# Moving the old-state products behind a unit's first scores, with new figures in the planner

## The chip, the cores and the metric

The kernel runs on one core of a Trainium2 chip. The metric is the device time in microseconds (us), median of the runs. TensorE is called PE, VectorE DVE, ScalarE ACT, GpSimd POOL; SP is the engine that issues most loads.

## The reference

A linear attention with a decaying state (4 batches, 8 heads, 768 steps, head size 48), then a gated projection with a convolution of five taps. Cut to what is computed:

```python
for t in range(S):
    cur = einsum('bhd,bhe->bhde', u[None] * kt, vt)
    y[:, :, t] = einsum('bhd,bhde->bhe', rt, state + cur)
    state = wt[:, :, :, None] * state + einsum('bhd,bhe->bhde', kt, vt)
# x = y with the heads side by side: (4, 768, 384)
for k in range(5):
    gate_pre += conv_w[k] * xp[:, k:k + S, :]
gate = 1 / (1 + exp(-gate_pre))
out = (gate * (x @ w_val)) @ w_out
```

## The kernel before

**Units.** Two heads form a pair, 16 pairs in all. A pair's 768 steps are cut into six chunks of 128 steps, each of two halves of 64. A unit is a pair, or part of one: 21 units, of which the first pair has two (two and four chunks), the pairs 1 to 11 one of six chunks each (units 2 to 12), and the last four pairs two each (four and two chunks).

**What a unit does.** `unit_front`: SP loads w, k and r (`rkw`); DVE scans the decays (`g` at L410, `f` at L437), and POOL (DVE in the first units) makes scaled keys `kh` and queries `q`; ACT makes `ru`, r times the bonus. `unit_state`: PE transposes the keys (L469), ACT copies them out (`kt`, L473), PE makes the state updates `pu` (L485) and those of the half chunks (L499), DVE chains them into states `st` (L524), PE adds the middle ones (L533), and ACT copies both into `z` (L546). `unit_scores`: PE multiplies the old states with the queries, `earlier` (L559), into the output bank `py`, and makes the scores in the bank `pp` (L580); DVE copies the wanted triangle and diagonal into `am` with two masked copies (L592). `unit_back`: PE adds `am` times v to `py`, `outputs` (L601), and ACT evacuates `py` into `xt` or, for every fourth pair, `ys` (L618). There is one bank pair for `pp` and one for `py`, so scores of one part wait for the masks of the part before, and `earlier` waits for the evacuation of the unit before.

**Parts.** A unit of six chunks makes scores and outputs in two parts of three chunks (`parts`); the smaller units have one part.

**The gate stage.** Whenever four pairs of a batch are done, two chunks of 384 steps of the gate stage are put in: taps on ACT and DVE (L695, L697), the two projections on PE (L636).

**The order.** All of this is written down as operations with an engine, a cost in ns and keys read and written (`r`, `w`). `Schedule.times` simulates the engines: at each step the engine that can start first takes, of its ready operations, the one with the longest rest of work behind it. `emit` then issues all of them by simulated start. So costs and keys decide only the order in which each engine gets its instructions; the waits between engines follow from the tiles. The key `py` in the scores' `r` is such an ordering: scores don't touch that bank. SP's operations are chained in the written order. `TensorClock` models PE's clock in the plan: double cost while it reckons PE as not warm, by the share of a model window in which PE was busy.

Of the kernel before, what the change touches and what calls it, by code (L numbers as in the profile page):

```python
# [19 lines left out]
B, H, S, D = 4, 8, 768, 48  # L20
# [34 lines left out]
def dve(n):  # L55
    return 75 + 1.042 * n


def scan(n):
    return 75 + 2.084 * n  # L60


def act(n, psum=False):
    return (60 if psum else 100) + 0.833 * n
# [10 lines left out]
class TensorClock:  # L75
# [6 lines left out]
        self.k, self.busy, self.warm = 0, 0.0, False  # L82

    def turn(self):
        self.warm = self.busy > (0.42 if self.warm else 0.9) * self.W
        self.k, self.busy = self.k + 1, 0.0

    def run(self, t, cost):
# [123 lines left out]
def rwkv_moe(ctx, tc, rkw, pad_d, vn_d, wv_d, wo_d, cw_d, small_d, out):  # L212
# [634 lines left out]
    op = ops.op  # L847
    units = [Unit(u) for u in range(NU)]

    def load(k, cost, fn, *args, w):  # L850
        op("SP", 470 * k, fn, *args, w=w)
        op("DMA", cost, None, w=w + ["loads"])

    def unit_v(u):
        load(1, 273 * units[u].n, load_v, u, w=[("vn", u % 4)])

    def unit_front(u, what="work"):
        a = units[u]
        n, i2, i3, rkk = a.n, u % 2, u % 3, ("rk", u % 4)
        rk_pad = [rkk, ("pad", u % 4)]  # L860
        N = n * L
        if what == "load":
            return load(2, 414 * n, load_rkw, u, w=[rkk])
        op("DVE", scan(N), a.scan_g, r=rk_pad + ["e1"] + ["e1b"] * (u > 0), w=["g"], port=True)
        op("DVE", 130, a.inverse, r=["g"], w=[("d1", i2)])
        op("Act", 110, a.totals, r=["g"], w=[("tot", u)])
        e, c = ("DVE", dve(N)) if u in DVE_KEYS else ("Pool", pool(N))
        op(e, c, a.keys, r=["g"] + rk_pad, w=[("kh", i3)], port=True)
        op("DVE", scan(N), a.scan_f, r=rk_pad + [("d1", i2)], w=[("f", i2)], port=True)
        e, c = ("DVE", dve(N)) if u in DVE_QUERIES else ("Pool", pool(N))  # L870
        op(e, c, a.queries, r=rk_pad + [("f", i2)], w=[("q", i3)], port=True)
        op("Act", act(N) + 188, a.guard, r=rk_pad + ["wmin"], w=[("ru", i3), ("low", u)])
        op("Act", act(N) + 93, a.bonus, r=rk_pad + ["masks"], w=[("ru", i3)])

    def unit_state(u):
        a = units[u]
        n, i2, i3 = a.n, u % 2, u % 3
        for j0 in range(0, n, 3):
            k = min(3, n - j0)
            pt = ("pm", ops.turn("pm", 2))  # L880
            op("PE", 104 * k, a.transpose, j0, r=[("kh", i3), "masks"], w=[pt])
            op("Act", act(112 * k, True), a.transposed, j0, r=[pt], w=[("kt", i2, j0)])
        kts = [("kt", i2, j0) for j0 in range(0, n, 3)]
        pu = ("pm", ops.turn("pm", 2))
        op("PE", 60 + 118 * a.slots, a.updates, r=kts + [("vn", u % 4)], w=[pu])
        ibk = ("ib", ib_key(u))
        op("Act", act(D * (n - 1)), a.decay, r=[("tot", u), "ibs"], w=[ibk])
        if a.late:
            op("Act", 150, a.carried, r=[("carry", a.p), pu], w=[pu])
        pu0 = ("pm", ops.turn("pm", 2))  # L890
        op("PE", 60 + 118 * n, a.halves, r=kts + [("vn", u % 4)], w=[pu0])
        op("DVE", scan(D * a.slots) + 60, a.chain, r=[pu, ibk], w=[("st", u % 4)] + [("carry", a.p)] * a.more)
        op("Act", act(D * n), a.state, 0, r=[("st", u % 4)], w=[("z", i2, 0)])
        op("PE", 60 + 40 * n, a.middle, r=[("st", u % 4), "masks"], w=[pu0])
        op("Act", act(D * n, True), a.state, 1, r=[pu0], w=[("z", i2, 1)])

    def unit_scores(u):
        a = units[u]
        n, i2, i3 = a.n, u % 2, u % 3
        op("PE", 60 + 232 * n, a.earlier, r=[("z", i2, 0), ("z", i2, 1), ("q", i3)], w=["py"])  # L900
        for i, j0 in enumerate(a.parts):
            op("PE", 60 + 240 * a.step, a.scores, i, w=["pp"],
               r=[("kh", i3), ("q", i3), ("ru", i3), ("rk", u % 4), "py"])
            N = 2 * a.step * 64
            for what in range(2):
                op("DVE", dve(N) + 60, a.mask, i, what, r=["pp", "masks"], w=[("a", i2, i)])

    def unit_back(u):
        a = units[u]
        i2, b, hp, n = u % 2, a.p // 4, a.hp, a.n  # L910
        for i, j0 in enumerate(a.parts):
            op("PE", 60 + 120 * a.step, a.outputs, i, r=[("vn", u % 4), ("a", i2, i)], w=["py"])
        own = [("x", b % 2, hp, c) for c in range(a.c0, a.c0 + n)]
        spare = [("xs", b % 2, c) for c in range(a.c0, a.c0 + n)]
# [88 lines left out]
    for u in range(NU):  # L1003
        a = units[u]
# [15 lines left out]
    op("Act", 2200, first_sigmoid, r=["warm"], boost=1e6)  # L1020
    for i in range(WARM):
        op("PE", 213, warm_up, 1, r=["warm"], w=[("pf", 0)], boost=-1e6)
    for i in range(4):
        op("Act", 600, load_pad, i, w=[("pad", i)])
        op("DMA", 240, None, w=[("pad", i)])
    unit_front(0, "load")
    load(1, 530, load_small, w=["masks"])
    unit_front(1, "load")
    unit_v(0)
    unit_front(2, "load")  # L1030
    unit_v(1)
    load(1, 50, load_taps, w=["cwr"])
    unit_front(3, "load")
    unit_v(2)
    unit_v(3)
# [24 lines left out]
    for u in range(NU):  # L1060
# [20 lines left out]
        p, c0, n = UNITS[u]  # L1081
# [79 lines left out]
```

## Time and profile before

| | us |
|---|---|
| median of 3 runs | 300.29 (298.99 to 301.29) |
| profiled execution | 301.02 |
| its span, first to last instruction | 299.2 |
| PE busy | 250.8 (84%) |
| DVE busy | 201.2 (67%) |
| ACT busy | 152.6 (51%) |
| POOL busy | 118.9 (40%) |

The profile is of one execution. Busy time is the time in which an engine had an instruction in hand; the ends of matmuls are modelled, so a busy PE is not PE at its peak. Two rows of PE matmuls can overlap. The granted clock is the share of full speed (2.4 GHz) that PE was given in a stretch. An idle time is put down to what ended it.

### The profile page before, as it was taken

How to read it: one execution, taken by the hardware profiler on the slowest of the kernel's cores; microseconds unless marked ns; L12 is line 12 of the kernel's file. 1: busy time of each engine (PE TensorE's matmuls, PEld its weight loads, DVE VectorE, ACT ScalarE, POOL GpSimd, SP SyncE). 2: the span in 40 equal slices, each digit the busy share in tenths (PEclk: the TensorE clock that was granted, in tenths of full speed). 3: DMA queues.
4: the chain of work that ended last, by engine and by line, in shares of the span. 5: the costliest groups of instructions: out<-in, count | busy, mean ns of one | idle time of the engine just before them, and what ended most of it. 6: DMA issues, size and time to landing. Idle time of an engine off the chain costs nothing. (4 is left out here: it accounts for less than half of the span.)

```text
span 299.2 us, 10120 instructions
## 1 busy us (share of the span) xinstructions
PE 250.8 (84%) x4411; PEld 213.2 (71%) x4411; DVE 201.2 (67%) x325; ACT 152.6 (51%) x347; POOL 118.9 (40%) x114
## 2 busy tenths in 40 slices
PE   7559988988689995899999899899689967966873
PEld 2448777767577874788788798699578956845762
DVE  2746867759985598788298797548597854577300
ACT  1645535353436484464485955634585743664211
POOL 8035226236327338705263771515263223061210
PEclk9655575555555899599999999979997995897798
DMA  7999976244542671552861533273222100100011
GB/s 146 174 182 301 261 160 121 45 82 83 110 92 53 110 129 36 104 137 59 149 151 37 110 76 113 61 149 92 65 57 79 56 15 3 61 22 26 26 53 64
DMA packets 13381, 28.81 MB, mean 96 GB/s; under 512 B 2192, under 2 KB 8208, under 8 KB 12208
## 3 DMA queue, kind: packets, MB, share of 16 engines
q1 hardware_dynamic: 8784, 21.58, 34.9%
q10 hardware_dynamic: 4544, 6.50, 7.7%
q8 instruction: 36, 0.59, 0.9%
q14 instruction: 17, 0.14, 0.2%
HBM read 22.17 MB, written 4.72 MB: 90 GB/s over the span
## 5 line engine op out<-in xcount | busy, mean ns | idle before, releaser
L697 DVE SCALAR_TENSOR_TENSOR acc<-xt,cw,acc 128x384 f32<-128x384 f32 (+1 forms) x108 | 61.4, 569 | 16.1 <-ACT acc L695 14.5
L410 DVE TENSOR_TENSOR_SCAN g<-rkw,e 112x774 f32<-112x774 f32 (+2 forms) x21 | 34.5, 1643 | 25.8 <-DMA rkw<-rkw 25.5
L592 DVE COPY_PREDICATED am<-small,pp 128x384 f32<-128x384 int32 (+2 forms) x64 | 37.4, 584 | 21.5 <-PE pp L580 21.4
L717 POOL TENSOR_TENSOR gl<-gt,gh 128x384 fp32r<-128x384 f32 (+1 forms) x27 | 27.1, 1002 | 61.8 <-ACT gh L713 61.8
L432 POOL TENSOR_TENSOR kh<-rkw,g 112x768 f32<-112x768 f32 (+2 forms) x19 | 28.1, 1477 | 40.3 <-PE pp L580 20.7
L446 POOL TENSOR_TENSOR q<-rkw,f 112x768 f32<-112x768 f32 (+2 forms) x20 | 28.3, 1413 | 31.4 <-DVE f L437 31.4
L559 PE MATMUL py<-q,z 48*48 48x64 f32 (+1 forms) x704 | 31.7, 253 | 8.7 <-ACT xt L618 5.7
L559 PEld LDWEIGHTS py<-q,z 48*48 48x48 f32 (+1 forms) x704 | 28.2, 156 | 13.1 <-ACT xt L618 6.3
L437 DVE TENSOR_TENSOR_SCAN f<-rkw,d 112x774 f32<-112x774 f32 (+2 forms) x21 | 32.5, 1548 | 0.2
L458 ACT ACTIVATE ru<-rkw,wmin 112x768 f32<-112x768 f32 (+2 forms) x21 | 16.4, 783 | 26.5 <-PE pp L580 15.7
L683 POOL TENSOR_TENSOR xl<-xt,xh 128x1152 fp32r<-128x1152 f32 (+2 forms) x11 | 21.6, 1968 | 18.7 <-ACT xh L679 17.3
L485 PE MATMUL pu<-vn,kt 128*64 128x48 f32 (+1 forms) x404 | 20.2, 253 | 10.0 <-DMA vn<-vn 5.2
L485 PEld LDWEIGHTS pu<-vn,kt 128*64 128x64 f32 (+1 forms) x404 | 17.4, 161 | 14.6 <-issue 7.1
L580 PE MATMUL pp<-q,kh 48*64 48x64 f32 x768 | 24.5, 258 | 3.1 <-issue 1.8
L710 DVE TENSOR_TENSOR gt<-gt,pv 128x384 f32<-128x384 f32 (+1 forms) x27 | 13.6, 502 | 19.5 <-PE pv L636 14.1
L636 PE MATMUL pv<-xh,wv_hi 128*128 128x384 f32 (+1 forms) x81 | 20.9, 369 | 6.0 <-DVE gt L710 4.7
L636 PE MATMUL po<-wo_hi,gh 128*128 128x384 f32 x72 | 22.1, 418 | 4.5 <-ACT ob L728 2.7
L601 PE MATMUL py<-am,vn 64*64 64x64 f32 (+1 forms) x768 | 22.4, 256 | 2.5 <-DVE am L592 2.5
L601 PEld LDWEIGHTS py<-am,vn 64*64 64x64 f32 (+1 forms) x768 | 18.0, 155 | 9.0 <-DVE am L592 5.1
L728 ACT COPY ob<-po 128x384 f32<-128x384 f32 x24 | 11.5, 479 | 24.8 <-PE po L636 19.2
L580 PEld LDWEIGHTS pp<-q,kh 48*64 48x64 f32 x768 | 19.5, 161 | 6.2 <-issue 3.6
L580 PE MATMUL pp<-ru,rkw 48*64 48x64 f32 x768 | 23.2, 252 | 0.0
(83 smaller groups left out, 477.1 us busy)
## 6 DMA issues: line engine op xcount, KB each, us to landing
rkw<-rkw SPq DMA_DIRECT2D x22, 435.9 KB, 7.2
out<-ob ACTq DMA_DIRECT2D x24, 192.0 KB, 2.0
vn<-vn SPq DMA_DIRECT2D x11, 288.0 KB, 6.2
rkw<-rkw SPq DMA_DIRECT2D x10, 290.8 KB, 5.1
rkw<-rkw SPq DMA_DIRECT2D x10, 145.7 KB, 2.9
xt<-wv SPq DMA_DIRECT2D x3, 384.0 KB, 10.3
raw_o<-wo SPq DMA_DIRECT2D x3, 384.0 KB, 13.3
vn<-vn SPq DMA_DIRECT2D x5, 192.0 KB, 2.9
```

The lines of the kernel that those rows point to most:

```text
L410: nc.vector.tensor_tensor_scan(self.g[:, 0:m][:, ::-1], w[:, 1 : m + 1][:, ::-1], e1[:, 0:m][:, ::-1], 0.0, op0=ALU.mult, op1=ALU.add,)
L432: eng.tensor_tensor(self.kh[:, 0:n, :], k, slots(self.g, n)[:, :, 1:WS], op=ALU.mult)
L437: nc.vector.tensor_tensor_scan(self.f[:, 0:m], rk(u)[:, 0, 0:m], d1[u % 2][:, 0:m], 0.0, op0=ALU.mult, op1=ALU.add)
L446: eng.tensor_tensor(self.q[:, 0:n, :], r, slots(self.f, n)[:, :, 0:L], op=ALU.mult)
L485: nc.tensor.matmul(self.pu[64 * h : 64 * h + rows, :, k], self.kt[:, c, 64 * h : 64 * h + rows], vn_t[u][:, c, 48 * h : 48 * h + 48], star ...
L559: nc.tensor.matmul(self.py[64 * h : 64 * h + m, j, 64 * c : 64 * c + 64], z_t[u % 2][ps, (2 * c + j) * D : (2 * c + j) * D + m], self.q[ps ...
L580: nc.tensor.matmul(pp[t, h, 128 * c + b : 128 * c + b + 64], lh[ps, j0 + c, t], rh[ps, j0 + c, t], start=True, stop=True,)
L592: nc.vector.copy_predicated(am, bm(mdia if what else mstr, step), p5[:, :, :, what, :])
L601: nc.tensor.matmul(self.py[64 * h : 64 * h + m, j, 64 * c : 64 * c + 64], vn_t[u][t, c, 48 * h : 48 * h + m], am[t, h, c, :], start=False, ...
L636: nc.tensor.matmul(ps, lh(a, cc), rh(bb, cc), start=(m == 0), stop=(m == 8))
L697: nc.vector.scalar_tensor_tensor(self.acc[j], x, w, self.acc[j], op0=ALU.mult, op1=ALU.add)
L717: nc.gpsimd.tensor_tensor(self.gl[:, j, 0:n], self.gt[:, j, 0:n], self.gh[:, j, 0:n].bitcast(F32), op=ALU.subtract)
```

## The change

In units of two parts the old-state products are written between the first and the last scores instead of ahead of both, and only the last scores carry the ordering key `py`. The outputs are written with the last part first. Six figures of the planner change: the busy share from which it reckons PE as warm (0.9 to 0.97), the time of a v load (273 to 230 ns a chunk), of an rkw load (414 to 727 ns a chunk), of a pad load (240 to 700 ns, now in one chain with the other loads), and of the copy of the states into z (340 to 705 ns for six chunks). The pad loads are written between the first units' loads instead of all ahead of them.

```diff
     def turn(self):
-        self.warm = self.busy > (0.42 if self.warm else 0.9) * self.W
+        self.warm = self.busy > (0.42 if self.warm else 0.97) * self.W
...
     def unit_v(u):
-        load(1, 273 * units[u].n, load_v, u, w=[("vn", u % 4)])
+        load(1, 230 * units[u].n, load_v, u, w=[("vn", u % 4)])
...
         if what == "load":
-            return load(2, 414 * n, load_rkw, u, w=[rkk])
+            return load(2, 727 * n, load_rkw, u, w=[rkk])
...
-        op("Act", act(D * n), a.state, 0, r=[("st", u % 4)], w=[("z", i2, 0)])
+        op("Act", 100 + 2.1 * D * n, a.state, 0, r=[("st", u % 4)], w=[("z", i2, 0)])
...
     def unit_scores(u):
         a = units[u]
         n, i2, i3 = a.n, u % 2, u % 3
-        op("PE", 60 + 232 * n, a.earlier, r=[("z", i2, 0), ("z", i2, 1), ("q", i3)], w=["py"])
         for i, j0 in enumerate(a.parts):
+            if i == len(a.parts) - 1:
+                op("PE", 60 + 232 * n, a.earlier, r=[("z", i2, 0), ("z", i2, 1), ("q", i3)], w=["py"])
             op("PE", 60 + 240 * a.step, a.scores, i, w=["pp"],
-               r=[("kh", i3), ("q", i3), ("ru", i3), ("rk", u % 4), "py"])
+               r=[("kh", i3), ("q", i3), ("ru", i3), ("rk", u % 4)] + ["py"] * (i == len(a.parts) - 1))
...
-        for i, j0 in enumerate(a.parts):
+        for i in reversed(range(len(a.parts))):
             op("PE", 60 + 120 * a.step, a.outputs, i, r=[("vn", u % 4), ("a", i2, i)], w=["py"])
...
-    for i in range(4):
+    def pad(i):
         op("Act", 600, load_pad, i, w=[("pad", i)])
-        op("DMA", 240, None, w=[("pad", i)])
+        op("DMA", 700, None, w=[("pad", i), "loads"])
+
+    pad(0)
     unit_front(0, "load")
     load(1, 530, load_small, w=["masks"])
+    pad(1)
     unit_front(1, "load")
     unit_v(0)
+    pad(2)
     unit_front(2, "load")
     unit_v(1)
     load(1, 50, load_taps, w=["cwr"])
+    pad(3)
     unit_front(3, "load")
```

## Rows read from the trace of the kernel before

**Rows 1.** The page, part 2: granted clock in 40 slices of 7.5 us, tenths.

```profile
PEclk9655575555555899599999999979997995897798
```

**Rows 2.** Stretches: us, each engine's busy us (instructions), granted clock, DMA share, GB/s.

```profile
0.00:20.00 20.00, 12.35 (x101) 6.82 (x103) 8.60 (x17) 6.97 (x19) 7.26 (x31) 0.76 0.97 167
...
40.00:42.00 2.00, 2.00 (x51) 1.88 (x48) 1.04 (x2) 0.00 (x0) 0.00 (x0) 0.73 1.01 196
...
46.00:99.00 53.00, 45.47 (x873) 39.17 (x866) 41.65 (x54) 25.49 (x52) 23.77 (x17) 0.50 0.47 88
64.00:84.00 20.00, 14.35 (x289) 12.36 (x290) 20.00 (x25) 10.36 (x22) 9.96 (x6) 0.50 0.61 113
...
126.00:192.00 66.00, 63.18 (x1347) 55.50 (x1346) 50.65 (x81) 40.01 (x85) 28.41 (x21) 1.00 0.43 98
240.00:299.00 59.00, 41.70 (x387) 35.61 (x383) 25.01 (x58) 22.66 (x56) 14.30 (x16) 0.84 0.10 34
```

**Rows 3.** PE's waits, 20 to 100 us: us in total, times, longest.

```profile
PE py L601 <- DVE am L592: 1.9, 1, 1.9
...
PE py L559 <- ACT xt L618: 1.0, 1, 1.0
PE py L559 <- ACT ys L618: 0.9, 1, 0.9
...
PE pp L580 <- DVE am L592: 0.5, 1, 0.5
```

**Rows 4.** PE's waits, 100 to 195 us.

```profile
PE py L559 <- ACT ys L618: 1.4, 2, 1.0
PE py L559 <- ACT xt L618: 0.9, 1, 0.9
...
PE pp L580 <- DVE am L592: 0.8, 2, 0.6
```

**Rows 5.** Timeline, 82 to 100 us: start, us, instruction, count, idle before.

```profile
82.91 2.50 PE L559 MATMUL py<-q,z 48*64 48x64 f32 x42 [0.93 <-ACT ys L618]
...
85.80 1.74 DVE L410 TENSOR_TENSOR_SCAN g<-rkw,e 112x774 f32<-112x774 f32 x1
85.90 0.89 PE L580 MATMUL pp<-ru,rkw 48*64 48x64 f32 x22
...
87.46 0.57 DVE L592 COPY_PREDICATED am<-small,pp 128x384 f32<-128x384 int32 x1
...
90.23 1.52 PE L485 MATMUL pu<-vn,kt 128*64 128x48 f32 x24 [0.53 <-ACT kt L473]
...
94.61 0.60 DVE L592 COPY_PREDICATED am<-small,pp 128x384 f32<-128x384 int32 x1 [2.05 <-PE pp L580]
...
95.62 0.58 DVE L592 COPY_PREDICATED am<-small,pp 128x384 f32<-128x384 int32 x1
...
96.30 0.91 PE L601 MATMUL py<-am,vn 64*64 64x64 f32 x24
...
99.81 1.43 PE L559 MATMUL py<-q,z 48*64 48x64 f32 x43
```

**Rows 6.** The page's DMA issues (KB each, us to landing), and one ACT copy.

```profile
rkw<-rkw SPq DMA_DIRECT2D x22, 435.9 KB, 7.2
...
rkw<-pad ACTq DMA_DIRECT2D x4, 145.3 KB, 7.8
...
87.82 0.71 ACT L546 COPY z<-st 112x288 f32<-112x288 f32 x1
```

**Rows 7.** Timeline of DVE around 20 us.

```profile
19.07 1.77 DVE L410 TENSOR_TENSOR_SCAN g<-rkw,e 112x774 f32<-112x774 f32 x1 [4.33 <-DMA rkw<-rkw]
20.76 0.42 DVE L592 COPY_PREDICATED am<-small,pp 128x256 f32<-128x256 int32 x1
```

**Rows 8.** Timeline of PE, two instructions behind a gap.

```profile
45.34 0.81 PE L580 MATMUL pp<-q,kh 48*64 48x64 f32 x20 [1.77 <-issue]
...
194.29 1.44 PE L559 MATMUL py<-q,z 48*64 48x64 f32 x28 [1.02 <-ACT ys L618]
```

## The prediction

> **What bounds the kernel now.** I read the page first. Its row of the granted TensorE clock stands at 5 to 7 tenths from the second slice to the thirteenth (to about 97 us), nearly always at the lower of the two levels, 1.2 GHz, and mostly at 9 behind it [rows 1]. So I cut the span into stretches. From 46 to 99 us PE is busy 45.47 of 53 us, all of it at 0.50; from 126 to 192 us it is busy 63.18 of 66 us at 1.00 [rows 2]. PE is the fullest engine in both, but they differ in what is left: 7.5 us of idle time in the first, 2.8 in the second. Inside the first lies 64 to 84 us, where VectorE has no idle time at all while PE has 5.65 us of it: there masks come late because DVE is full. After 240 us PE is busy 41.70 of 59 us; that is mostly the last batch's gate and projection, which the new order does not touch.
>
> Then I asked what PE waited for. From 20 to 100 us the idle time is split over many small waits: the products with the old states (L559) wait 1.0 + 0.9 us for an evacuation of the unit before, the scores 0.5 us for a mask, the outputs 1.9 us for a mask [rows 3]. From 100 to 195 us L559 waits 1.4 + 0.9 us and the scores 0.8 us [rows 4].
>
> Last, one round of the loop from unit to unit, at the low clock [rows 5]. L559 of one unit starts at 82.91, after 0.93 us of waiting for ACT's evacuation. The first scores follow and end at 86.79. Their first mask starts on DVE only at 87.46, because a scan g of 1.74 us stands before it. The next unit's updates fill PE at 90.23. The masks of the second scores start at 94.61 and 95.62, the outputs at 96.30, and the next L559 at 99.81. The round takes 16.9 us, and two pairs of masks and one evacuation stand in it one behind the other.
>
> **The change part by part.**
>
> *L559 moves behind the first scores.* In a unit of six chunks it is 44 matmuls, which pass 24 + 24 matmuls of scores on PE; no DMA goes with them, and on the other queues nothing is passed. Units of two or four chunks have one part, so their order stays. Two waits should go. L559 no longer meets an unfinished evacuation, since the first scores, which don't write py, run in that time: about 1.3 us of them (85.4 to 86.79) against waits of about 1 us [rows 5]. And the second scores no longer meet unfinished masks, since L559 now runs in that time: 2.50 us at the low clock, 1.43 us at the high one, against a pair of masks of 2 x 0.58 us. The terms: from 20 to 100 us 1.0 + 0.9 + 0.5 = 2.4 us [rows 3]; from 100 to 195 us 1.4 + 0.9 + 0.8 = 3.1 us [rows 4], less the 1.0 at 194.29, whose 28 matmuls show a unit of four chunks [rows 8]: 2.1 us. Together 4.5 us. The lower bound is 0 (the same idle time comes back at the next wait); the upper is all of PE's idle time in the two stretches, 7.5 + 2.8 = 10.3 us. I take 4.5, the waits that the new order names, because PE is the fullest engine around them.
>
> *Both parts' outputs now come after the last scores, the second part first.* Before, the first part's outputs (0.9 us at the low clock) could run while the second masks were made. Now all 48 matmuls wait for the last mask, which ends at 96.20, 1.6 us after the masks could begin; with the way back to PE that is some 1.7 us per unit [rows 5], and the evacuation and the next L559 are queued behind. The work that hides it is the next unit's transposes, updates, halves and middle products; the updates alone are 1.52 us at the low clock [rows 5], and the four together over 3. I take 0. If that cover stood somewhere else, it would be 11 units x 1.7 = 19 us, the other bound.
>
> *Loads reckoned dearer, v cheaper, one copy dearer.* The planner's rkw load goes to 727 ns a chunk, 4.36 us for a unit of six whose two transfers of 435.9 KB landed in 7.2 us each; z from st goes to 100 + 2.1 x 288 = 705 ns, which the trace has at 0.71 [rows 6]. No work comes with this, only another order. SP keeps the written order of its loads, since the planner chains them, so no load passes another. What it can do is seen at the start: DVE waited 4.33 us for unit 2's load with unit 0's masks queued behind that scan [rows 7]. A plan that knows the load to be late puts the masks first, which takes one mask, 0.42 us, out of the way of unit 1's states, and unit 0's outputs as well. Between 0 and 1.1 us; I take 0.5.
>
> *Pads.* The four pad transfers of 145.3 KB are issued from ACT [rows 6]. Their issues wait for nothing in either plan, so I cost the new place at 0. If two of them really went behind the first unit's loads, these would land earlier by 2 x 145.3 KB at the 167 GB/s of that stretch [rows 2], 1.7 us: the upper bound.
>
> *A stricter clock in the planner* only makes it reckon with slow matmuls for longer, and that reorders every engine, in the tail too. No row prices it. The nearest are PE's single waits that an order can make or remove, the longest of them 1.9 us outside the start [rows 3]; so 1.9 us either way, and I take 0.
>
> Sum: 4.5 + 0.5 = 5.0 us off the profiled execution's 301.02 (a span of 299.2 and 1.8 around it), 296.0. That execution stood 0.73 us above the median of the runs, 300.29, so the forecast is 300.29 - 5.0 = **295.3 us**.
>
> **The rivals.**
>
> *The clock rises early.* PE was granted 0.73 in 40 to 42 us [rows 2], behind a stretch of scores and updates, and lost it in a gap that ended at 45.34 [rows 8]. Scores, L559 and scores in one piece make a longer dense stretch in every unit. At the high level L559 would fall from 2.50 to 1.43 us [rows 5], PE would bound 46 to 99 us no longer, and DVE, with 41.65 us of work there [rows 2], would: some 45 us in place of 53, a gain of 8 where the first case has 2.4. That gives 300.29 - 8 - 2.1 - 0.5 = 289.7, about 290. Against it: 45.47 busy us out of 53 did not raise the clock, and DVE's full stretch will go on making gaps. The Trainium skill (TensorE: Matmul & The Clock Gate, "What's actually happening") has the throttled state as the default, which activity releases. By that rule denser work would bring this case; the trace agrees at 40 us and speaks against counting on it by the 53 us at 0.50.
>
> *Nothing net.* The waits of L559 and the scores go, and the same idle time stands at the outputs or, from 64 to 84 us, behind DVE. Or the planner finds the first scores ready no sooner than the old products, and the change hardly does what it says. Either way about 299.5.
>
> *Slower: the outputs lose their cover.* If the plan puts the next unit's state work ahead of the second scores, little stands between these and the outputs, and evacuation, L559 and everything after slide. For it speak the 1.9 us that the outputs wait already [rows 3], and the 1.74 us scan that DVE ran before a mask [rows 5]. From 5.0 / 11 = 0.45 us uncovered per unit on, the gain is gone. With the 1.7 us uncovered in half of the 11 units it is 9.4 - 5.0 = 4.4 us slower than before, about 305. Against it: both waits of that kind in the two stretches add up to little over 2 us, since something nearly always stood between.
>
> **How the numbers follow.** Waits removed, clock as before (292 to 298): 0.42. Clock early (284 to 292): 0.20. Nothing net (298 to 302): 0.18. Slower (302.5 to 310): 0.20. The time is that of the first, 295.3. A range of 285 to 304 leaves out the lowest end of the clock case (0.03) and the upper part of the slow one (0.13), and takes in the bounds of the small terms. About 1%, 3 us, can be told from no change. Faster than 297.3 are 0.8 of the first case and the whole clock case: 0.54. Slower than 303.3 is nearly all of the last: 0.20. Within it: 0.26.
>
> **What would show it.** Right: from 20 to 195 us L559 waits for an evacuation only in units of four chunks or fewer, the scores' waits for masks vanish, and the outputs' waits for masks stay under 3 us. The clock case: a granted clock above 0.6 over much of 46 to 99 us. Slower: outputs waiting over 8 us for masks. I am wrong in the place, whatever the total, if the difference arises after 240 us, where I put none, or before 20 us beyond half a microsecond.

## The result and the profile after

The changed kernel takes 289.65 us (median of 4 runs, 286.49 to 293.44) beside 300.79 us of the kernel before (4 runs, 298.99 to 305.29): a ratio of 0.958 [0.946, 0.969]. (A ratio compares undisturbed runs alone, so it need not be the quotient of the two medians.) A second measurement of the same file gave 287.38 us and 0.964 [0.953, 0.975]. The forecast was 295.3 us; the time lies inside its range, and the gain is about twice the one forecast.

The profiled execution took 288.46 us, its span 286.7 us. The page's first two parts, of the changed kernel:

```profile
PE 237.6 (83%) x4411; PEld 204.3 (71%) x4411; DVE 201.5 (70%) x325; ACT 152.6 (53%) x347; POOL 121.9 (43%) x114
...
PEclk9855555596557999999699999999986999978998
```

No engine has less to do: DVE is busy 201.5 us (201.2 before) and ACT 152.6 us, as before. PE is busy 237.6 us in place of 250.8, with the same matmuls, because more of them ran at the high clock. The row of the granted clock reaches its run of 9s one slice earlier than in [rows 1].

To see where the time went, both spans are cut where the same work begins: at the old-state products (L559) of unit 5 and of unit 13. The views of stretches, first of the kernel before, then of the changed one (columns as in [rows 2]: us, then busy us and instructions of PE, weight load, DVE, ACT and POOL, granted clock, DMA share, GB/s):

```profile
0.00:82.90 82.90, 65.50 (x1108) 52.44 (x1108) 57.19 (x81) 37.49 (x84) 32.86 (x47) 0.58 0.74 151
82.90:194.30 111.40, 101.90 (x2121) 88.14 (x2121) 84.42 (x128) 65.10 (x135) 54.86 (x35) 0.90 0.44 94
194.30:299.20 104.90, 83.44 (x1184) 72.59 (x1184) 59.58 (x117) 50.00 (x129) 31.21 (x32) 0.88 0.19 55
82.90:299.20 216.30, 185.34 (x3303) 160.73 (x3303) 144.00 (x245) 115.10 (x263) 86.07 (x67) 0.89 0.32 75
```

```profile
0.00:82.90 82.90, 58.60 (x1107) 46.84 (x1107) 55.08 (x81) 37.02 (x83) 32.15 (x47) 0.63 0.80 158
82.90:187.70 104.80, 97.19 (x2079) 85.73 (x2079) 88.83 (x127) 63.71 (x131) 58.30 (x36) 0.93 0.45 97
187.70:286.70 99.00, 81.82 (x1227) 71.70 (x1227) 57.55 (x118) 51.87 (x134) 31.45 (x33) 0.92 0.18 56
82.90:286.70 203.80, 179.01 (x3306) 157.43 (x3306) 146.38 (x244) 115.57 (x265) 89.75 (x68) 0.93 0.32 77
```

Three things are to be seen. Unit 5 begins at 82.9 us in both, with 1107 and 1108 matmuls done: the first third gained nothing. The whole 12.5 us lie behind it: 6.6 us up to unit 13, 5.9 us after it. (At unit 13 the changed kernel has some 40 matmuls of the next unit's state work still ahead of it, 2079 against 2121; that is over 1 us which the middle owes the tail, so the split between the two is rough, while the sum is not: 3303 and 3306 matmuls.) And of these 12.5 us half is idle time, half is busy time: PE sat idle 216.30 - 185.34 = 31.0 us before and 203.80 - 179.01 = 24.8 us after, 6.2 us less; it was busy 6.3 us less, at a granted clock of 0.93 in place of 0.89.

**What became of the waits.** PE's waits between unit 5 and unit 13 of the kernel before, then of the changed one (us in total, times, longest; L559's for xt and the scores' for masks are as in [rows 4]):

```profile
PE pu L533 <- DVE st L524: 2.7, 1, 2.7
PE py L559 <- ACT ys L618: 2.3, 3, 1.0
PE py L601 <- DVE am L592: 0.6, 1, 0.6
```

```profile
PE pp L580 <- DVE am L592: 4.5, 2, 2.7
PE py L559 <- ACT z L546: 2.8, 2, 2.6
PE pu L485 <- ACT kt L473: 1.6, 3, 0.5
PE py L601 <- DVE am L592: 0.5, 1, 0.5
```

No old-state product waits for an evacuation there any more, and the outputs wait as little as before. But the scores' wait for masks did not vanish: it is 4.5 us in two pieces. (The view counts a wait with the instruction that it delays. Of the waits for ys and for z, 0.93 and 2.56 us stand right before unit 5's own old-state products, at 82.91 and 82.88 us, and so ahead of the cut; the middle itself has 0.2 us for z.) All of PE's idle time in this stretch fell only from 9.5 us (111.40 - 101.90) to 7.6 us (104.80 - 97.19). One unit of the changed kernel on PE shows the new order and one of the two pieces:

```profile
105.19 0.56 PE L580 MATMUL pp<-q,kh 48*64 48x64 f32 x24
...
106.46 1.49 PE L559 MATMUL py<-q,z 48*64 48x64 f32 x44
107.95 0.90 PE L485 MATMUL pu<-vn,kt 128*64 128x48 f32 x24
108.78 0.90 PE L499 MATMUL pu<-vn,kt 64*64 64x48 f32 x24
111.46 0.58 PE L580 MATMUL pp<-q,kh 48*64 48x64 f32 x24 [1.79 <-DVE am L592]
```

First scores, old-state products, next unit's updates and halves, second scores (and, at 114.63 us, both parts' outputs in one row of 48): the move is done as the diff says. Even with 1.49 + 0.90 + 0.90 us of work between the two scores, PE waited 1.79 us for the masks. DVE's timeline shows what stood before them, here and at the longer piece, 2.72 us at 137.37 us; two rows of POOL stand ahead of it:

```profile
105.09 3.22 POOL L683 TENSOR_TENSOR xl<-xt,xh 128x1152 fp32r<-128x1152 f32 x1 [2.98 <-ACT xh L679]
108.26 3.02 POOL L446 TENSOR_TENSOR q<-rkw,f 112x768 f32<-112x768 f32 x1
...
106.30 0.59 DVE L592 COPY_PREDICATED am<-small,pp 128x384 f32<-128x384 int32 x1
106.78 3.16 DVE L410 TENSOR_TENSOR_SCAN g<-rkw,e 112x774 f32<-112x774 f32 x1
...
110.83 0.57 DVE L592 COPY_PREDICATED am<-small,pp 128x384 f32<-128x384 int32 x1
...
136.17 0.55 DVE L710 TENSOR_TENSOR gt<-gt,pv 128x384 f32<-128x384 f32 x1 [2.85 <-ACT gt L700]
136.65 0.58 DVE L592 COPY_PREDICATED am<-small,pp 128x384 f32<-128x384 int32 x1
```

The two masked copies of one part are 4.5 us apart, with a scan of 3.16 us and steps of the gate stage between; and at 136 us the second copy is queued behind a gate step that itself waits 2.85 us for ACT. The same scan took 1.74 us in [rows 5], with nothing on POOL beside it; here xl and q run on POOL all through it.

**What a wait costs.** The granted clock shows where the other half came from. The stretches around two of the changed kernel's longest waits behind 100 us, and the timeline's rows of these waits:

```profile
131.00:138.00 7.00, 4.28 (x140) 3.79 (x142) 3.54 (x7) 2.17 (x6) 3.46 (x3) 0.99 0.31 78
138.00:145.00 7.00, 7.00 (x105) 6.26 (x102) 5.29 (x7) 4.49 (x7) 5.92 (x3) 0.52 0.38 89
206.00:213.00 7.00, 4.61 (x83) 3.82 (x82) 6.67 (x13) 5.82 (x13) 4.94 (x5) 1.00 0.22 59
213.00:220.00 7.00, 6.70 (x102) 6.07 (x102) 3.69 (x6) 2.61 (x7) 1.20 (x2) 0.51 0.06 20
```

```profile
137.37 0.58 PE L580 MATMUL pp<-q,kh 48*64 48x64 f32 x24 [2.72 <-DVE am L592]
...
213.30 1.75 PE L559 MATMUL py<-q,z 48*64 48x64 f32 x28 [2.02 <-ACT z L546]
```

Ahead of 138 us PE had the high level, 2.4 GHz (0.99), and sat idle 2.72 us of 7; in the 7 us behind, it was busy without a break at 0.52, nearly all at the low level of 1.2 GHz. The same stands around 213 us (1.00, a wait of 2.02 us, then 0.51). The kernel before has it too, with another wait: at 119.17 us the middle products wait 2.66 us for states, and 119.5 to 126.5 us runs at 0.51. A single long wait thus stands ahead of a slow stretch, and where the one brings the other, it costs its own length and half of that stretch's busy time, here, by an estimate, (1 - 0.52) x 7.00 = 3.4 us. The Trainium skill (TensorE: Matmul & The Clock Gate, "HAM oscillation — how this bites in real kernels") tells of a kernel whose every wait for data is followed by matmuls at the low clock; both traces agree at these places. But it does not come behind every wait here: in the kernel before one of 2.63 us, at 212.99 us, has 213 to 220 us behind it at 1.00, though PE was busy only 4.37 of the 7 us ahead. And in a second execution of the changed kernel (below) the wait for masks near 137 us, 2.13 us there, has 7 us behind it at 1.00. So which waits bring a slow stretch differs between executions of one program.

**The tail.** The last outputs (L601) of the kernel before start at 260.15 us, with 324 of the gate stage's 459 projection matmuls (L636) done, and 38.6 us are left behind their end. Those of the changed kernel start at 267.23 us, with 387 done, and 19.0 us are left. So the changed plan runs 63 more of them ahead of the last outputs. That stretch has units of one part only, in which the move changes nothing by itself; the planner, which plans all of the program anew, placed them so.

### The profile page after: what moved, and what is told of

It reads as the page before. It is cut to its first block, busy times and chain, and to the rows that moved or that the text cites. A ratio compares the mean times of both kernels' runs of the same rounds, so it can differ in the third digit from the quotient of the medians.

```text
span 286.7 us, 10120 instructions
## 1 busy us (share of the span) xinstructions
PE 237.6 (83%) x4411; PEld 204.3 (71%) x4411; DVE 201.5 (70%) x325; ACT 152.6 (53%) x347; POOL 121.9 (43%) x114
## 4 chain that ended last, share of the span: by engine, by line
PE 58%; ACT 12%; DVE 10%; DMA 10%; issue 4%; ACTq 3%; SPq 1%; POOL 1%; DVEq 0%; POOLq 0%
PE po L636 14%; PE pv L636 11%; PE pp L580 8%; PE py L559 8%; DMA rkw<-rkw 5%; PE pu L485 5%; PE pu L499 4%; PE py L601 4%; DVE acc L697 3%; DMA vn<-vn 3%; PE pt L469 3%; ACTq L627 3%; PE pu L533 2%; DMA xt<-ys 2%; DVE am L592 2%
## 5 line engine op out<-in xcount | busy, mean ns | idle before, releaser
L717 POOL TENSOR_TENSOR gl<-gt,gh 128x384 fp32r<-128x384 f32 (+1 forms) x27 | 29.0, 1076 | 49.8 <-ACT gh L713 49.8
L410 DVE TENSOR_TENSOR_SCAN g<-rkw,e 112x774 f32<-112x774 f32 (+2 forms) x21 | 38.4, 1831 | 11.6 <-DMA rkw<-rkw 11.5
L559 PE MATMUL py<-q,z 48*48 48x64 f32 (+1 forms) x704 | 29.9, 245 | 11.9 <-ACT z L546 6.3
L432 POOL TENSOR_TENSOR kh<-rkw,g 112x768 f32<-112x768 f32 (+2 forms) x19 | 26.8, 1410 | 30.1 <-PE pp L580 15.5
L559 PEld LDWEIGHTS py<-q,z 48*48 48x48 f32 (+1 forms) x704 | 26.7, 149 | 16.6 <-ACT z L546 7.9
L683 POOL TENSOR_TENSOR xl<-xt,xh 128x1152 fp32r<-128x1152 f32 (+2 forms) x11 | 23.2, 2110 | 22.1 <-ACT xh L679 21.1
L580 PE MATMUL pp<-q,kh 48*64 48x64 f32 x768 | 22.8, 253 | 4.5 <-DVE am L592 4.5
L473 ACT COPY kt<-pt 128x336 f32<-128x336 f32 (+2 forms) x37 | 14.7, 401 | 16.8 <-PE pt L469 13.1
L636 PE MATMUL pv<-xh,wv_hi 128*128 128x384 f32 (+1 forms) x81 | 20.4, 361 | 3.4 <-DVE gt L710 1.9
L636 PE MATMUL po<-wo_hi,gh 128*128 128x384 f32 x72 | 20.4, 395 | 1.9 <-ACT ob L728 1.3
L469 PE MATMUL pt<-small,kh 112*128 112x112 f32 x96 | 19.0, 314 | 1.5 <-DVE kh L432 1.5
```

The costliest lines, as they stand in the source:

```text
L410: nc.vector.tensor_tensor_scan(self.g[:, 0:m][:, ::-1], w[:, 1 : m + 1][:, ::-1], e1[:, 0:m][:, ::-1], 0.0, op0=ALU.mult, op1=ALU.add,)
L432: eng.tensor_tensor(self.kh[:, 0:n, :], k, slots(self.g, n)[:, :, 1:WS], op=ALU.mult)
L469: nc.tensor.transpose(pt[:, j, :], self.kh[:, j0 + j, :], ident[0:112, 0:112])
L559: nc.tensor.matmul(self.py[64 * h : 64 * h + m, j, 64 * c : 64 * c + 64], z_t[u % 2][ps, (2 * c + j) * D : (2 * c + j) * D + m], self.q[ps ...
L580: nc.tensor.matmul(pp[t, h, 128 * c + b : 128 * c + b + 64], lh[ps, j0 + c, t], rh[ps, j0 + c, t], start=True, stop=True,)
L636: nc.tensor.matmul(ps, lh(a, cc), rh(bb, cc), start=(m == 0), stop=(m == 8))
```

## The experiments

In each, the table of a profiled execution is cut at unit 5 and unit 13 as above. All tables stand together behind the last experiment.

**The new written order alone** (the kernel before, with the two hunks of scores and outputs, and all figures of before):

```diff
-        op("PE", 60 + 232 * n, a.earlier, r=[("z", i2, 0), ("z", i2, 1), ("q", i3)], w=["py"])
         for i, j0 in enumerate(a.parts):
+            if i == len(a.parts) - 1:
+                op("PE", 60 + 232 * n, a.earlier, r=[("z", i2, 0), ("z", i2, 1), ("q", i3)], w=["py"])
...
-               r=[("kh", i3), ("q", i3), ("ru", i3), ("rk", u % 4), "py"])
+               r=[("kh", i3), ("q", i3), ("ru", i3), ("rk", u % 4)] + ["py"] * (i == len(a.parts) - 1))
...
-        for i, j0 in enumerate(a.parts):
+        for i in reversed(range(len(a.parts))):
```

> The kernel before with only the new written order (old-state products between the scores, outputs reversed, py key on the last scores); all planner figures as before. Theory A (the new order makes denser PE stretches, and these raise the clock): about 290 us, PE busy 240 us or less, the granted clock above 0.6 over 46 to 99 us. Theory B (the planner's new figures carry the gain): 298 to 303 us, PE busy about 250. Theory C (either part only reshuffles, and the gain is of the pair): between, 294 to 300.

Measured: 294.14 us (292.52 to 298.25, 4 runs) beside 300.07, ratio 0.981 [0.970, 0.992]. The order by itself is worth some 6 us, about the prediction's 5.0, but not in the prediction's place; the time is at the low end of theory C. Unit 5 begins at 77.1 us, 5.8 us earlier, and behind it nothing is left of a gain (215.7 us in place of 216.3):

```profile
0.00:77.10 77.10, 60.24 (x1108) 48.33 (x1108) 49.51 (x75) 36.32 (x80) 30.57 (x45) 0.62 0.77 161
77.10:184.50 107.40, 94.45 (x2079) 83.55 (x2078) 95.36 (x135) 63.16 (x133) 51.98 (x37) 0.94 0.50 105
184.50:292.80 108.30, 88.06 (x1227) 77.96 (x1227) 59.31 (x116) 52.79 (x135) 33.74 (x34) 0.84 0.15 47
```

DVE has done 75 instructions by unit 5, where the kernel before has done 81, and 7.7 us less of work (49.51 and 57.19): this plan puts less work for later units into the crowded start, and no run shows whether that is the reason. What the middle wins, the tail gives back, at a clock of 0.84.

**The figures and the pads' place alone** (the kernel before with the other hunks of the diff):

```diff
-        self.warm = self.busy > (0.42 if self.warm else 0.9) * self.W
+        self.warm = self.busy > (0.42 if self.warm else 0.97) * self.W
...
-            return load(2, 414 * n, load_rkw, u, w=[rkk])
+            return load(2, 727 * n, load_rkw, u, w=[rkk])
...
-        op("Act", act(D * n), a.state, 0, r=[("st", u % 4)], w=[("z", i2, 0)])
+        op("Act", 100 + 2.1 * D * n, a.state, 0, r=[("st", u % 4)], w=[("z", i2, 0)])
...
```

> The kernel before with only the planner's six new figures and the pads written between the loads; order of scores and outputs as before. Theory A: 299 to 303 us, PE busy about 250, 46 to 99 us at the low clock. Theory B: about 290 us with PE busy near 238. Theory C: 294 to 300.

Measured: 301.31 us (296.49 to 303.45, 10 runs) beside 300.07, ratio 1.019 [1.006, 1.032]. The figures alone bring nothing or lose a little. (The profiled execution, 296.49 us, is the fastest of the ten.) Together with the order they bring 5 us more than the order alone: the two parts don't add up, since each makes the planner write another program.

**The reversed outputs alone** (the kernel before, one line):

```diff
-        for i, j0 in enumerate(a.parts):
+        for i in reversed(range(len(a.parts))):
```

> The kernel before with the outputs alone reversed (last part first, both behind the last masks); old-state products first, figures as before. If waiting for the last masks costs what the slower rival of the prediction said (1.7 us in half of the 11 units), about 305 to 310 us with the outputs waiting over 8 us for masks. If the cover holds, as the prediction took it: 299 to 303 us, these waits under 4 us.

Measured: 301.7 us (one execution) beside a median of 300.07. From 20 to 195 us the outputs wait 3.6 us for masks, where the kernel before has 2.5 us; the bound of 19 us that the prediction kept for lost cover is far off:

```profile
PE py L601 <- DVE am L592: 3.6, 3, 2.5
```

**The planner's clock share set back** (the changed kernel):

```diff
-        self.warm = self.busy > (0.42 if self.warm else 0.97) * self.W
+        self.warm = self.busy > (0.42 if self.warm else 0.9) * self.W
```

> The changed kernel with the planner's clock share back at 0.9, everything else as changed. If the stricter share carries the gain: 298 us or more, PE busy about 250 us. If the order and the loads do: 288 to 292 us, PE busy about 238.

Measured: 286.12 us (one execution). The two programs hold the same instructions in the same order on every engine, so this is one more execution of the changed kernel. With all else in place the stricter clock changes nothing, as the prediction had taken it (0).

**The changed kernel again**, unchanged, for its spread:

> The changed kernel once more, beside the kernel before, for the spread of time over granted clock in executions of one instruction order. Over 14 executions of the kernel before, a microsecond more at the low clock goes with 0.35 us more time (mean 110.4 us low, 300.4 us). Theory A (all of the gain is the clock): the changed kernel lies on that line, so at its mean of some 92 us low it should take 300.4 - 0.35 x 18 = 294. Theory D (clock and shorter loop both): it lies 4 to 6 us under that line, at 288 to 291 us.

Measured: 287.38 us (283.3 to 290.98, 4 runs) beside 300.01, ratio 0.964 [0.953, 0.975]. With the run above and those of the result, nine executions of this program lie between 283.3 and 293.44 us. The profiled one, 283.3 us, has PE idle 23.7 us behind unit 5, as the others of this program do (23.7 to 24.8), and the higher clock (0.95). At these four executions' mean of 89 us at the low clock (span x 2 x (1 - granted clock)) theory A's line gives 293 us; they lie 5.5 us under it, so the clock is not all of the gain.

**The load figures and the pads as before** (the changed kernel):

```diff
-        load(1, 230 * units[u].n, load_v, u, w=[("vn", u % 4)])
+        load(1, 273 * units[u].n, load_v, u, w=[("vn", u % 4)])
...
-            return load(2, 727 * n, load_rkw, u, w=[rkk])
+            return load(2, 414 * n, load_rkw, u, w=[rkk])
...
-        op("DMA", 700, None, w=[("pad", i), "loads"])
+        op("DMA", 240, None, w=[("pad", i)])
...
-    pad(0)
+    for i in range(4):
+        pad(i)
...
```

> The changed kernel with the planner's load figures and the place of the pads as before (414 and 273 ns a chunk, pads first); new order, new copy figure and clock share kept. The order alone took about 294 us and the full change about 290. If the load figures make that difference: 293 to 296 us. If they only cost time at the start (its first units ran 1 to 3 us later than before): 286 to 288 us. If the copy's figure does it: 288 to 291 us.

Measured: 301.27 us (297.31 to 302.7, 4 runs) beside 300.01. The whole gain is gone, with the move in place, and the time lies above all three forecasts. In the profiled execution unit 5 begins at 85.4 us, the middle takes 112.5 us and the tail 100.7. So the load and pad figures, with the pads' place, are needed, though no instruction got cheaper by them. They were set back together, so which of them counts is not shown.

**More warming matmuls**, in the kernel before and in the changed one. They compute nothing that is used; they raise the clock in the first 46 us:

```diff
-WARM = 16
+WARM = 48
```

> The kernel before with 48 instead of 16 warming matmuls that fill PE's planned idle time in the first units; they compute nothing that is used. Nothing else changes in what is computed. Theory clock (the low clock from 20 to 97 us costs time): where the granted clock holds above 0.8 over 20 to 46 us, the units get there sooner and the time falls by 3 to 8 us, to 292 to 297. Theory loads (the first 46 us go by the loads whatever the clock): within 2 us of 300, with a higher granted clock.

> The changed kernel with 48 instead of 16 warming matmuls. Theory clock: a higher granted clock over 10 to 46 us and 283 to 287 us. Theory loads: 288 to 292 us with a higher granted clock. If the matmuls get in the way of the first units' work: above 292 us.

Measured: the kernel before 300.11 us (10 runs; ratio 1.002 [0.991, 1.012]), the changed one 290.0 us (4 runs; 0.972 [0.962, 0.982] against the kernel before). The start of the kernel before with 48 of them (an execution of 306.37 us, the longest of the ten):

```profile
0.00:20.00 20.00, 14.71 (x104) 7.09 (x106) 7.57 (x16) 6.03 (x16) 7.24 (x31) 0.91 0.97 156
20.00:46.00 26.00, 17.61 (x367) 14.34 (x369) 16.43 (x20) 12.97 (x30) 7.74 (x5) 0.84 1.00 230
...
0.00:88.10 88.10, 67.14 (x1136) 51.23 (x1140) 58.16 (x81) 37.75 (x84) 31.53 (x47) 0.69 0.73 142
```

The clock from 20 to 46 us is 0.84; with 16 of them it was 0.57. Unit 5 begins no sooner: at 88.1 us here, at 83.0 us in the changed kernel, whose clock over that stretch went from 0.63 to 0.75. The DMA share is 0.97 and 1.00 there, and DVE waits 15.0 us for loads of rkw in the first 46 us (10.8 us with 16 warming matmuls). In the kernel before, the added matmuls are all that differs in the order of any engine, so there a higher clock in the first 46 us buys nothing. In the changed kernel they also made the planner write another order (369 projection matmuls ahead of the last outputs), so that run does not test the clock alone.

**The gate stage held back** (the changed kernel; the planner gets a weight that puts the gate stage of the last two batches behind the units, so that 324 projection matmuls stand ahead of the last outputs, as in the kernel before):

```diff
...
-        self.bias.append(boost)
+        self.bias.append(boost + self.base)
...
+        ops.base = -30000.0 if f.b >= 2 and not f.tail else 0.0
...
```

> The changed kernel with the gate stage of the last two batches put behind the units' work in the planner's choice (its weight lowered by 30000 ns); nothing else. In the order that comes out, 324 of the 459 projection matmuls stand before the last outputs on PE, as in the kernel before, where the changed kernel has 387. Theory tail (about half of the gain lies behind unit 13, because more of the gate stage is done between the last small units): the stretch from unit 13's L559 to the end goes from 99 back to about 104 us, some 33 us remain behind the last outputs instead of 19, and the time is 292 to 295 us. Theory clock (the gain is the granted clock alone): 287 to 290 us.

Measured: 300.76 us (296.51 to 305.36, 10 runs) beside 299.29, ratio 1.006 [1.000, 1.013]. The time lies above both forecasts. Up to 194 us the order of every engine is the changed kernel's, so the middle keeps its gain, and what differs is the tail: it is 12.8 us longer than that of the changed kernel, and 6.9 us longer than that of the kernel before, though as many matmuls are ahead:

```profile
84.30:187.90 103.60, 96.42 (x2079) 85.10 (x2079) 89.24 (x128) 63.81 (x131) 58.44 (x36) 0.94 0.45 98
187.90:299.70 111.80, 86.33 (x1227) 75.69 (x1227) 57.54 (x117) 51.39 (x135) 31.71 (x33) 0.87 0.16 50
```

With less of the gate stage between them (126 of its matmuls from unit 13's to the last unit's old-state products, 180 in the changed kernel and 126 in the kernel before), PE has 25.4 us of idle time in the tail, and the low clock comes behind the longer waits. The longest stands at 243.84 us; the stretches ahead of it and behind:

```profile
243.84 0.67 PE L485 MATMUL pu<-vn,kt 128*64 128x48 f32 x8 [4.24 <-ACT kt L473]
```

```profile
237.00:243.50 6.50, 2.60 (x31) 2.28 (x29) 1.99 (x5) 2.71 (x8) 3.16 (x3) 0.99 0.04 10
243.50:250.00 6.50, 6.16 (x76) 5.78 (x77) 2.92 (x8) 2.53 (x9) 1.32 (x2) 0.50 0.02 4
```

**The move alone taken back** (the changed kernel with L559 ahead of all scores and the key on all of them; figures, pads and reversed outputs stay):

```diff
+        op("PE", 60 + 232 * n, a.earlier, r=[("z", i2, 0), ("z", i2, 1), ("q", i3)], w=["py"])
         for i, j0 in enumerate(a.parts):
-            if i == len(a.parts) - 1:
-                op("PE", 60 + 232 * n, a.earlier, r=[("z", i2, 0), ("z", i2, 1), ("q", i3)], w=["py"])
...
-               r=[("kh", i3), ("q", i3), ("ru", i3), ("rk", u % 4)] + ["py"] * (i == len(a.parts) - 1))
+               r=[("kh", i3), ("q", i3), ("ru", i3), ("rk", u % 4), "py"])
```

> The changed kernel with the old-state products back ahead of all scores and the ordering key back on all of them; the reversed outputs and all new figures kept. If the move carries the stretch from unit 5's to unit 13's L559 (111.4 us before, 104.8 changed): 109 to 111 us there, waits of L559 for evacuations again 3 us or more, and 299 to 302 us in all. If the figures and the reversed outputs carry it: 104 to 106 us there and 288 to 292 us.

Measured: 304.17 us (302.8 to 307.57, 4 runs) beside 299.29, ratio 1.028 [1.016, 1.040]. So without the move the rest of the change loses some 5 us. The middle takes 113.7 us, with 18 more projection matmuls done in it than the changed kernel has. Both the middle and the whole are longer than either theory had them. PE's longest waits there:

```profile
PE po L636 <- ACT ob L728: 4.0, 3, 3.3
PE pu L485 <- ACT kt L473: 3.5, 3, 2.3
PE py L559 <- ACT xt L618: 1.7, 2, 1.1
```

L559 waits for evacuations again, 1.7 us, but the larger waits are others.

**The last units put off a little** (the changed kernel, with a weight that lowers the last eight units in the planner's choice; 396 projection matmuls stand ahead of the last outputs):

```diff
...
+        ops.base = -20000.0 if u >= 13 else 0.0
...
```

> The changed kernel with the last eight units' work put lower in the planner's choice by 20000 ns, so that 396 instead of 387 projection matmuls stand before the last outputs. Theory tail: 1 to 2 us shorter behind unit 13, 286 to 288 us. If the units now come too late for the last gate chunks: 290 us or more.

Measured: 289.56 us (285.85 to 291.93, 4 runs) beside 299.29, ratio 0.968 [0.953, 0.983]: no better than the changed kernel. Nine more matmuls in place gain nothing that can be told.

**Clock share and copy figure as before** (the changed kernel; what stays new is the order, the load and pad figures and the pads' place):

```diff
-        self.warm = self.busy > (0.42 if self.warm else 0.97) * self.W
+        self.warm = self.busy > (0.42 if self.warm else 0.9) * self.W
...
-        op("Act", 100 + 2.1 * D * n, a.state, 0, r=[("st", u % 4)], w=[("z", i2, 0)])
+        op("Act", act(D * n), a.state, 0, r=[("st", u % 4)], w=[("z", i2, 0)])
```

> The changed kernel with two of its new figures set back, the planner's clock share (0.9) and the copy of the states (act(D n) in place of 705 ns for six chunks); new are the written order, the load and pad figures and the pads' place. Its plan has 378 of the 459 gate-projection matmuls ahead of the last outputs, 9 fewer than the changed kernel's 387. If the gain is the move plus how much of the gate stage runs between the last small units: the middle stretch (unit 5's to unit 13's old-state products) 102 to 107 us as in the changed kernel, the stretch behind it about 1.5 us longer than there, in all 287 to 292. If the copy's figure is what the plan needs to put z ahead of its readers: waits of the old-state products for z over 6 us in the middle stretch, and 295 or more.

Measured: 291.86 us (288.87 to 297.2, 4 runs) beside 300.73, ratio 0.969 [0.961, 0.977]. Most of the gain is there. L559 waits 8.7 us for z by the view (1.7 us of it at unit 5's own, ahead of the cut), as the copy's old figure let one expect, yet the middle is only 1.9 us longer and the tail no longer:

```profile
PE py L559 <- ACT z L546: 8.7, 4, 4.8
```

**All tables together.** Worked out from the profiled executions: us of the three stretches; behind unit 5 PE's idle time (length less busy time) and the granted clock; PE's idle time in the tail; and the projection matmuls, of 459, ahead of the last outputs.

| kernel | to unit 5 | to unit 13 | tail | behind unit 5: idle, clock | tail idle | ahead |
|---|---|---|---|---|---|---|
| changed | 82.9 | 104.8 | 99.0 | 24.8, 0.93 | 17.2 | 387 |
| changed, again | 82.7 | 101.6 | 97.2 | 23.7, 0.95 | 17.0 | 387 |
| clock share back (same program) | 81.9 | 105.4 | 97.0 | 23.7, 0.92 | 17.1 | 387 |
| last units put off | 84.0 | 106.7 | 97.3 | 24.5, 0.92 | 17.4 | 396 |
| clock share and copy back | 83.4 | 106.7 | 98.8 | 26.7, 0.92 | 17.2 | 378 |
| changed, 48 warming | 83.0 | 107.2 | 95.0 | 28.7, 0.96 | 18.6 | 369 |
| load figures back | 85.4 | 112.5 | 100.7 | 30.8, 0.89 | 17.9 | 369 |
| order alone | 77.1 | 107.4 | 108.3 | 33.2, 0.89 | 20.2 | 360 |
| figures alone | 84.8 | 108.9 | 101.0 | 33.3, 0.92 | 20.2 | 351 |
| move alone back | 83.6 | 113.7 | 103.7 | 32.6, 0.88 | 20.0 | 351 |
| outputs reversed alone | 84.4 | 110.6 | 104.8 | 34.9, 0.92 | 25.0 | 333 |
| before | 82.9 | 111.4 | 104.9 | 31.0, 0.89 | 21.5 | 324 |
| before, 48 warming | 88.1 | 112.5 | 103.9 | 30.8, 0.89 | 21.3 | 324 |
| gate stage held back | 84.3 | 103.6 | 111.8 | 32.7, 0.90 | 25.4 | 324 |

Two columns are to be read. The idle time of the tail goes with the last column: 17 to 19 us where 369 or more matmuls are ahead, 20 us at 351 and 360, over 21 us at 324 and 333. And behind unit 5 the kernels at 286 to 292 us have 23.7 to 28.7 us of idle time, all others 30.8 to 34.9.

How far one execution can be trusted is to be seen too. Up to 240 us the order of "last units put off" is the changed kernel's as well. So five executions of one order up to unit 13 (its own three, this one and "gate stage held back") took 101.6 to 106.7 us in the middle, and the order of the kernel before took 111.4 and 112.5 us. In the tail the changed kernel's three took 97.0 to 99.0 us, those of the kernel before's order 104.9 and 103.9 us.

## Why the prediction was right, and where it was not

**What bounds it.** That PE was the fullest engine from 100 us on was right. For the first 83 us it was wrong to count PE's waits as time. The term of 2.4 us from 20 to 100 us [rows 3] bought nothing by unit 5: PE was busy 6.9 us less in the changed kernel (65.50 and 58.60) and idle 6.9 us more. The trace hinted at it, with DVE at 20.00 of 20 us [rows 2] and 10.8 us of DVE's waits for loads of rkw in the first 46 us. The order alone, though, did reach unit 5 by 5.8 us sooner; with either half of the new figures added that is gone (83.4 us with those of the loads and pads, 85.4 us with the other two).

**The 4.5 us of named waits.** The mechanism is half right. The evacuations' waits of six-chunk units, 1.3 us of the term, are gone in the middle, at the price of nothing at the outputs. But the second scores' wait for masks, 0.8 us [rows 4], became 4.5 us: the masks of the first scores stood behind a scan and behind a gate step on DVE, as the rows above show. The step that failed is the cover: work on PE between the two scores does not help when DVE's queue is what the masks wait for. And one unit of six chunks still waits for its evacuation, 2.24 us at 65.34 us. So two of the three signs that the prediction gave for its first case failed (evacuations, masks), and the third held: the outputs waited 0.8 us for masks from 20 to 195 us, well under 3. The middle's term, 2.1 us, stands against 1.9 us less of idle time, but with other waits in the balance than the ones named, and the clock came on top.

**The outputs' cover, taken at 0.** Right, for the reason given in most units only. With the reversed outputs alone their waits grow to 3.6 us. In the changed kernel the next unit's updates and halves stand in between in six of the nine units from 4 to 12, as the prediction said; in units 6, 7 and 11 they stand ahead of the second scores (as in the unit shown above), which was the condition of the slower case, and there nine projection matmuls of the gate stage and little else are cover enough. The sign of the slower case, outputs that wait over 8 us for masks from 20 to 195 us, came in no run.

**The start, taken at 0.5 us.** Wrong. DVE still takes unit 2's scan ahead of unit 0's masks, 1 us later than in [rows 7]:

```profile
20.07 1.77 DVE L410 TENSOR_TENSOR_SCAN g<-rkw,e 112x774 f32<-112x774 f32 x1 [4.66 <-DMA rkw<-rkw]
21.76 0.42 DVE L592 COPY_PREDICATED am<-small,pp 128x256 f32<-128x256 int32 x1
```

Unit 1's old-state products start at 27.68 us in place of 24.83. PE's waits for v come to 6.8 us in the first 83 us, in place of 5.2. By unit 5 the delay is made up.

**The clock rival.** Its sign came: 46 to 99 us ran at 0.68 in place of 0.50 [rows 2]. Its price of 8 us there did not: in these 53 us PE was busy 41.95 us in place of 45.47 [rows 2], but idle 11.05 us in place of 7.53, and unit 6 begins at 97.09 us in place of 99.81 [rows 5], a gain of 2.7. That its time, 289.7 us, is close to the one measured is luck. Where the clock did pay is behind unit 5: 6.3 us less of busy time for the same matmuls. The prediction priced the clock only as a long stretch that rises as one, and did not see that it also dips behind single waits, for a few microseconds at a time. [Rows 1] shows such dips behind 100 us, each in one or two slices; the prediction passed over them.

**After 240 us, where the prediction put none.** This is the step that failed most, and by the prediction's own sign it was wrong in the place. The tail behind unit 13 is 5.9 us shorter. From unit 18's old-state products on, at 239.81 us before and at 245.33 us now, 41.4 us are left in place of 59.4, since more of the gate stage is done ahead of them. The test with the gate stage held back shows that 12.8 us of tail can hang on where the planner puts the gate stage: enough to give back all of the gain with the move in place. Its tail is longer than the kernel before's too, with as many matmuls ahead, so how much of the 5.9 us comes from their place stays open. "The last batch's gate and projection, which the new order does not touch" was true of the written order and not of the plan made from it.

**The size.** 12.5 us in the profiled execution, against 5.0: 0 in the start (0.5 and 2.4 forecast), 6.6 up to unit 13 (2.1 forecast), 5.9 behind it (0 forecast). So the total came within the range by other terms than the sum's, which is luck.

**What is shown and what is not.** Shown: neither part alone brings all of it (order alone 294.14, figures alone 301.31, move taken back 304.17, load and pad figures taken back 301.27); the place of the gate stage alone can move the tail by as much as the whole gain; a higher clock in the first 46 us of the kernel before is worth nothing. Only seen, in the traces: that the low clock begins behind long waits, and not behind each. Over 39 executions of the kernel before, an execution is 0.31 us longer for each us at the low clock (correlation 0.89); by that, 5.7 us of the 11.6 us between the means of these and of the changed kernel's nine would go with the clock, about the half that the busy time shows. But no run changed the clock behind unit 5 and nothing else. Open: why the load and pad figures, with the pads' place, turn the plan from 301 to 288 us. They shift ready times throughout the plan, and no run separates one shift from another. Not tried: the move without the reversed outputs.

## To carry to other kernels

Where a planner writes the program, an edit of one ordering or one cost is an edit of the whole program: look in the new order for what moved in stretches that the edit doesn't touch, above all the tail, before any wait is counted as saved. Count PE's waits as time only where PE, not a load or another engine, sets the end; before work on PE is taken as cover for a wait, look at the queue of the engine that ends it. And look behind each long wait for a slow stretch, which may cost as much again. Compare two kernels at points of equal work, with idle and busy time apart; the same total came here from terms that a comparison by clock time would have mixed.

## What the runs showed of the hardware

A single wait of 2.02 us with PE at the high level was followed by 7 us at 0.51. Ahead of it PE was busy 4.61 of 7 us. Most other dips behind 100 us, in both kernels, begin within 1.3 us of a single wait of 1.0 to 3.4 us, while another wait of 2.63 us, with PE busy 4.37 of the 7 us ahead, was followed by 7 us at 1.00. In two executions of one program the same wait (2.72 and 2.13 us) was followed by 0.52 in the one and by 1.00 in the other. A scan of 112x774 on DVE took 1.74 to 1.77 us with POOL idle beside it, and 3.16 to 4.18 us in the three places where POOL ran q and xl all through it. A clock held high through the first 46 us by matmuls that compute nothing (0.84 in place of 0.57 from 20 to 46 us) left the whole time where it was, 300.11 us beside 300.01. And one program on one core, measured on more than one chip, spreads by 10 us from execution to execution (283.3 to 293.44 us for the changed kernel), with the granted clock between 0.842 and 0.856 in the three that were profiled.
